# A tuned gated-convolution and two-MLP kernel on one core: other PSUM banks for transposes, later places for splits, sums and one block's convolution

## The chip, the cores and the metric

The kernel runs on one core of one Trainium2 chip. The metric is the time of one execution on the device in microseconds, smaller being better. Times are medians over several runs. The engines are PE (TensorE, matrix products and transposes), ACT (ScalarE), DVE (VectorE), POOL (GpSimd) and SP (SyncE, which issues the transfers).

## The reference

There are 8192 tokens (2 sequences of 4096) of 192 channels. Three steps follow one another, all in float32:

```python
# 1. dynamic convolution: 8 heads of 24 channels, 7 taps, weights by softmax over the taps
w = exp(weight_gen - max); w = w / (sum(w) + 1e-9)
x = einsum('bshk,bskhg->bshg', w, x_unfolded)       # this token and the 6 before it
# 2. layer 1: RMS norm, gated MLP, d_ff 1536
xn = x / sqrt(mean(x * x) + 1e-6) * rms_g
g = xn @ w_gate
y = (g * sigmoid(g) * (xn @ w_val)) @ w_out
# 3. layer 2: MLP, d_ff 2048
h = y @ w_in
z = (h * sigmoid(1.702 * h)) @ w_out
```

## The kernel before

The tokens are worked in 16 blocks of 512. For each block the program does the convolution with tokens on the partitions (on DVE, 13 operations over 128x768 elements, prepared by the softmax, whose exponential runs on ACT), the norm, and a transpose to channels on the partitions (TensorE, against an identity). Both MLPs then run with channels on the partitions.

Each float32 factor is split into a high and a low part of the shorter type fp32r (`h` and `l`; for x and y `xh`, `xl`, and for channels 128 to 191 `xsh`, `xsl`), and products are sums of several matmuls. Each matmul covers 64 rows of the array, and matmuls of the upper and of the lower rows go in pairs, side by side. The weights are split on the chip in the early part ("decode", lines 82 to 121).

The work is cut into **units**. Unit (1,b,m) makes 128 hidden columns of layer 1 for block b: it fills the PSUM banks `pg` and `pv`, ACT computes silu of `pg` into `p` (L401), DVE multiplies it with `pv` (L405), ACT casts the product to `h` (L406), DVE subtracts to get `l` (L409). Layer 1 has 12 such units per block. Unit (2,b,i) makes 256 hidden columns of layer 2: banks `ph` twice, ACT computes gelu of each to `h` (L422) and again to `p` (L423), DVE subtracts to `l` (L429). There are 8 per block. A unit's products with the second weights (D1 in layer 1, D2 in layer 2, each five matmul pairs) are added to the block's two sums `a` and `b` one or two units later, inside the matmul list of that later unit. A layer 1 unit so has nine pairs of its own and five for D1, 14; a layer 2 unit nine and ten, 19.

PSUM has 8 banks. Four form the pool `pu`, tag "u", for units and for the x transposes, so that a bank comes round after two units. The other four form `pacc`, for the sums: tags "a" and "b", two buffers each. When a bank passes from one row half to the other, an empty instruction on POOL relays the word (L331).

**Y(b)** takes layer 1's finished sums out of PSUM and splits them into `yh`, `yl`, `ysh`, `ysl`, the input of layer 2: four operations on ACT (L455 to L460) and three on DVE (L458, L459, L461). **Z(b)** takes out layer 2's sums and sends them to memory.

From block 2 on the order of units is: (1,b,4) to (1,b,11), then (1,b+1,0) to (1,b+1,3), then (2,b,0) to (2,b,7). At unit (1,b,10) the transposes of x(b+1) are issued, Y(b) falls to unit (1,b+1,1) and Z(b) to (1,b+1,5). Blocks 0 and 1 are interleaved. Block 14's layer 1 sums end, and all of block 15's layer 1 runs, ahead of block 14's layer 2.

Each engine works through its instructions in the order of the program. The first 24 units (AUTO) are ordered by the framework's scheduler, the rest stand as they are written. Convolution and weight decode are cut into small steps with costs and due times, and `some` deals them out between the parts of a unit:

```python
            for f in after:
                f()
            todo = [share(k, i) / 2 for k in (0, 1)]
            some(todo)
            second()
            some(todo)
            third()
```

`after` holds Y or Z. `second` is, in layer 1, product and cast, and `third` the subtraction; in layer 2 they are the two subtractions.

## Time and profile before

| | |
|---|---|
| median of 3 runs | 1325.36 us (1324.98 to 1326.92) |
| profiled execution | 1325.58 us, of which the span of instructions 1323.8 us |
| busy share of the span | PE 94%, DVE 60%, ACT 52%, POOL 2% |
| mean granted clock of TensorE | 0.988 |
| chain that ended last | PE 78%, DVE 12%, ACT 6% |

The busy share counts the time in which an engine has an instruction at work. The chain follows the work back from the last instruction, each step to what released it. The granted clock is a share of 2.4 GHz; 0.5 is the lower level, 1.2 GHz. In timeline rows a bracket gives how long the engine stood idle ahead of the instruction and what it waited for.

### The profile page before, as it was taken

What the parts mean: (1) busy time and instruction counts of PE and PEld (TensorE: products, weight loads), DVE (VectorE), ACT (ScalarE), POOL (GpSimd) and SP (SyncE); (2) the same over time, 40 slices, a digit from 0 to 9 for tenths busy, and PEclk for the clock granted to TensorE, in tenths of its full rate; (3) what the DMA queues carried; (4) which work ended last, traced back from release to release, by engine and by line L of the source; (5) the groups of instructions that cost most, each with busy time, mean ns of one, the idle gap of its engine ahead of it and who ended that gap; (6) DMA issues with size and microseconds to landing.
All of it is one profiled execution on the core that took longest, in us unless ns stands there. A gap on an engine that the chain in (4) does not pass through costs nothing.

```text
span 1323.8 us, 26554 instructions
## 1 busy us (share of the span) xinstructions
PE 1243.9 (94%) x10472; PEld 1131.5 (85%) x10472; DVE 788.7 (60%) x1286; ACT 691.8 (52%) x1350; POOL 31.5 (2%) x52
## 2 busy tenths in 40 slices
PE   1778899999999999999999999999999999999998
PEld 0567798889899898989989898998989899898897
DVE  8996575766655656565565656555466655645332
ACT  3564565465554555555555555545554555554453
POOL 3000000000000000000000000000000000000000
PEclk9989899999999999999999999999999999999999
DMA  6672121001001010100101000010100001000000
GB/s 232 218 241 86 54 67 65 32 1 43 2 1 53 1 43 1 43 2 1 53 2 43 1 26 18 1 54 1 43 1 12 32 1 44 1 13 2 1 14 12
DMA packets 16812, 51.70 MB, mean 39 GB/s; under 512 B 2096, under 2 KB 2480, under 8 KB 16560
## 3 DMA queue, kind: packets, MB, share of 16 engines
q1 hardware_dynamic: 16688, 50.01, 11.6%
q8 instruction: 82, 1.34, 0.4%
q14 instruction: 42, 0.34, 0.1%
HBM read 43.71 MB, written 6.29 MB: 38 GB/s over the span
## 4 chain that ended last, share of the span: by engine, by line
PE 78%; DVE 12%; ACT 6%; issue 2%; DMA 1%; POOL 0%; DVEq 0%; SPq 0%; POOLq 0%
PE a L316 21%; PE ph L316 18%; PE b L316 14%; PE pv L316 14%; PE pg L316 12%; DVE p L405 3%; DVE xr L229 2%; DVE acc L237 2%; ACT h L406 1%; ACT L422 1%; ACT h L422 1%; DVE dec_a L105 1%; DVE yt L458 1%; DVE ysl L461 1%; ACT ysh L460 1%
## 5 line engine op out<-in xcount | busy, mean ns | idle before, releaser
L316 PE MATMUL a<-h,o 64*128 64x512 f32 x1792 | 526.4, 395 | 4.2 <-POOLq L331 3.9
L316 PEld LDWEIGHTS a<-h,o 64*128 64x128 f32 x1792 | 330.2, 186 | 18.7 <-ACT p L401 4.2
L316 PE MATMUL b<-h,o 64*128 64x512 f32 x896 | 316.5, 397 | 9.3 <-ACT h L422 9.3
L316 PE MATMUL a<-l,o 64*128 64x512 f32 x896 | 318.1, 397 | 7.3 <-DVE l L429 7.2
L316 PE MATMUL b<-l,o 64*128 64x512 f32 x896 | 313.6, 395 | 2.8 <-DVE l L409 2.8
L429 DVE TENSOR_TENSOR l<-p,h 128x512 fp32r<-128x512 f32 x256 | 176.5, 690 | 221.7 <-ACT p L423 221.3
L422 ACT ACTIVATE h<-ph 128x512 fp32r<-128x512 f32 x256 | 153.5, 600 | 239.0 <-PE ph L316 237.0
L316 PE MATMUL pv<-xh,w 64*128 64x512 f32 x768 | 246.6, 401 | 17.1 <-DVE p L405 15.7
L316 PE MATMUL pg<-xh,w 64*128 64x512 f32 x768 | 254.2, 403 | 6.4 <-ACT xh L298 3.9
L316 PE MATMUL ph<-yh,w 64*128 64x512 f32 x1024 | 251.5, 395 | 0.0
L406 ACT CAST h<-p 128x512 fp32r<-128x512 f32 x192 | 119.0, 620 | 178.8 <-DVE p L405 178.8
L405 DVE TENSOR_TENSOR p<-p,pv 128x512 f32<-128x512 f32 x192 | 131.4, 684 | 111.0 <-PE a L316 77.9
L409 DVE TENSOR_TENSOR l<-p,h 128x512 fp32r<-128x512 f32 x192 | 132.8, 692 | 102.4 <-ACT h L406 102.4
L401 ACT ACTIVATE p<-pg 128x512 f32<-128x512 f32 x192 | 114.5, 597 | 149.0 <-PE pg L316 87.1
L316 PEld LDWEIGHTS b<-h,o 64*128 64x128 f32 x896 | 166.2, 186 | 20.1 <-ACT h L422 14.6
L316 PEld LDWEIGHTS a<-l,o 64*128 64x128 f32 x896 | 166.9, 186 | 17.1 <-DVE l L429 12.9
L316 PEld LDWEIGHTS b<-l,o 64*128 64x128 f32 x896 | 166.6, 186 | 10.5 <-DVE l L409 4.3
L316 PEld LDWEIGHTS pv<-xh,w 64*128 64x128 f32 x768 | 139.1, 187 | 36.7 <-DVE p L405 30.5
L316 PE MATMUL ph<-yl,w 64*128 64x512 f32 x512 | 163.7, 394 | 0.0
L316 PEld LDWEIGHTS ph<-yh,w 64*128 64x128 f32 x1024 | 152.6, 186 | 12.6 <-issue 0.2
L316 PEld LDWEIGHTS pg<-xh,w 64*128 64x128 f32 x768 | 142.0, 187 | 16.9 <-ACT xh L298 4.7
L423 ACT ACTIVATE p<-ph 128x512 f32<-128x512 f32 x256 | 152.4, 595 | 0.0
(81 smaller groups left out, 2211.8 us busy)
## 6 DMA issues: line engine op xcount, KB each, us to landing
x<-in_xp SPq DMA_DIRECT2D x14, 960.0 KB, 4.9
st<-in_w SPq DMA_DIRECT2D x20, 384.0 KB, 3.9
zt<-in_w SPq DMA_DIRECT2D x20, 384.0 KB, 3.8
st<-in_wo SPq DMA_DIRECT2D x14, 384.0 KB, 3.5
zt<-in_wo SPq DMA_DIRECT2D x14, 384.0 KB, 3.8
out_z<-za SPq DMA_DIRECT2D x16, 256.0 KB, 2.0
out_z<-zb SPq DMA_DIRECT2D x16, 128.0 KB, 2.3
x<-in_xp SPq DMA_DIRECT2D x1, 1344.0 KB, 5.9
```

The lines of the kernel that those rows point to most:

```text
L105: nc.vector.scalar_tensor_tensor(out=ai, in0=ai, scalar=3, in1=t["s"], op0=ALU.logical_shift_left, op1=ALU.bitwise_or)
L229: eng.tensor_tensor(out=dst.rearrange("p (q g) -> p q g", g=GRP), in0=x[:, k * D + a * GRP:k * D + e * GRP].rearrange("p (q g) -> p q g", ...
L237: eng.tensor_tensor(out=total[:, r], in0=total[:, r], in1=prod[:, r], op=ALU.add)
L316: ins = nc.tensor.matmul(ps[:, :N], w[rows], x[rows, :N], start=start, stop=stop)
L401: nc.scalar.activation(out=p[:, :N], in_=pg[:, :N], func=AF.Silu)
L405: nc.vector.tensor_tensor(out=p[:, :N], in0=p[:, :N], in1=pv[:, :N], op=ALU.mult)
L406: nc.scalar.copy(h[:, :N], p[:, :N])
L409: nc.vector.tensor_tensor(out=l[:, :N], in0=p[:, :N], in1=h[:, :N].bitcast(F32), op=ALU.subtract)
L422: nc.scalar.activation(out=h[:, :N], in_=ps[j][:, :N], func=AF.Gelu_apprx_sigmoid)
L423: nc.scalar.activation(out=p[:, :N], in_=ps[j][:, :N], func=AF.Gelu_apprx_sigmoid)
L429: nc.vector.tensor_tensor(out=l[:, :N], in0=p[:, :N], in1=h[:, :N].bitcast(F32), op=ALU.subtract)
L458: nc.vector.tensor_tensor(out=t[:, :N], in0=t[:, :N], in1=pb[:, :N], op=ALU.add)
```

## The change

- The four banks of the sums get fixed tags `a0`, `b0`, `a1`, `b1` by the parity of the block (`sums`), and the x transposes write there (`ax_`, `bx_`) instead of into unit banks.
- `transpose_x` issues the transposes at once and returns the split (4 ACT and 4 DVE operations, 2 and 2 for the first blocks), which comes behind the unit's product, cast and subtraction. So do Y and Z. Block 1's split stays where it was.
- From block 2 on, D2(b,0), layer 2's first sums, come one unit later: unit (2,b,1) has 14 pairs, (2,b,2) has 24. In the last unit of all, D2(13) is taken in rather than done alone after it.
- Block 2's x load, softmax and convolution start at unit (1,1,6) instead of (1,1,0).
- Block 0's convolution is no longer shared with POOL (SHARED): DVE does 768 elements instead of 624.
- Z's copy of `a` goes from DVE to ACT.

```diff
 
 BLOCKS = [4] * 16
 GROUPS = [(0, 1), (1, 2), (2, 4), (4, 7), (7, 10), (10, 13), (13, 16)]
-SHARED = {0: 6}
+SHARED = {}
 AHEAD = 4
 LAG = 6
 LAG2 = 3
...
     stg = early.enter_context(tc.tile_pool(name="stg", bufs=NST))
     dec = early.enter_context(tc.tile_pool(name="dec", bufs=3))
     pu = ctx.enter_context(tc.tile_pool(name="pu", bufs=4, space=PSUM))
-    pacc = ctx.enter_context(tc.tile_pool(name="pacc", bufs=2, space=PSUM))
+    pacc = ctx.enter_context(tc.tile_pool(name="pacc", bufs=1, space=PSUM))
 
     ident = const.tile([P, P], F32, name="ident")
     half = const.tile([P, TM], F32, name="half")
...
         xrow[b] = xr
         return ops
 
+    def sums(b, nm):
+
+        return [pacc.tile([P, NM], F32, tag=f"{n}{b % 2}", name=f"{n}{nm}{b}") for n in "ab"]
+
     def transpose_x(b, halves=False):
 
 
...
         l = xtp.tile([P, NM], F32R, tag="xl", name=f"xl{b}")
         sh = xtp.tile([P, NM], F32R, tag="xsh", name=f"xsh{b}")
         sl = xtp.tile([P, NM], F32R, tag="xsl", name=f"xsl{b}")
-        pa = pu.tile([P, NM], F32, tag="u", name=f"pa{b}")
-        pb = pu.tile([P, NM], F32, tag="u", name=f"pb{b}")
+        pa, pb = sums(b, "x_")
+        xT[b] = (h, l, sh, sl)
         if halves:
 
             for c in range(2):
...
                 for j in range(T):
                     nc.tensor.transpose(ps[:, j * P:(j + 1) * P], xr[:, j, c * P:(c + 1) * P], ident)
             parts = [(c, ps[:, :N], None) for c, ps in enumerate((pa, pb))]
-        for c, ps, i in parts:
-            h_, l_ = ((h, l), (sh, sl))[c]
-            h_, l_ = h_[:, :N], l_[:, :N]
-            if i is not None:
-                h_, l_ = (v.rearrange("p (j i t) -> p j i t", i=2, t=DR)[:, :, i] for v in (h_, l_))
-            nc.scalar.activation(out=h_, in_=ps, func=AF.Identity, scale=gt[:, c:c + 1])
-            nc.vector.scalar_tensor_tensor(out=l_, in0=ps, scalar=gt[:, c:c + 1],
-                                           in1=h_.bitcast(F32), op0=ALU.mult, op1=ALU.subtract)
-        xT[b] = (h, l, sh, sl)
+
+        def split():
+            for c, ps, i in parts:
+                h_, l_ = ((h, l), (sh, sl))[c]
+                h_, l_ = h_[:, :N], l_[:, :N]
+                if i is not None:
+                    h_, l_ = (v.rearrange("p (j i t) -> p j i t", i=2, t=DR)[:, :, i] for v in (h_, l_))
+                nc.scalar.activation(out=h_, in_=ps, func=AF.Identity, scale=gt[:, c:c + 1])
+                nc.vector.scalar_tensor_tensor(out=l_, in0=ps, scalar=gt[:, c:c + 1],
+                                               in1=h_.bitcast(F32), op0=ALU.mult, op1=ALU.subtract)
+        return split
 
 
     parts = [(sph, spl)]
...
 
     def D1(b, m):
         if m == 0:
-            acc1[b] = (pacc.tile([P, NM], F32, tag="a", name=f"a1_{b}"),
-                       pacc.tile([P, NM], F32, tag="b", name=f"b1_{b}"))
+            acc1[b] = sums(b, "1_")
         return (acc1[b], O1[m], m, M1, BLOCKS[b] * P, hl1.pop((b, m))), (lambda: Y(b)) if m == M1 - 1 else None
 
     def D2(b, m):
         if m == 0:
-            acc2[b] = (pacc.tile([P, NM], F32, tag="a", name=f"a2_{b}"),
-                       pacc.tile([P, NM], F32, tag="b", name=f"b2_{b}"))
+            acc2[b] = sums(b, "2_")
         return (acc2[b], O2[m], m, M2, BLOCKS[b] * P, hl2.pop((b, m))), (lambda: Z(b)) if m == M2 - 1 else None
 
     def Y(b):
...
         za = zp.tile([P, NM], F32, tag="za", name=f"za{b}")
         zb = zp.tile([P, NM], F32, tag="zb", name=f"zb{b}")[0:DR]
         nc.scalar.copy(zb[:, :N], pb[DR:P, :N])
-        nc.vector.tensor_copy(za[:, :N], pa[:, :N])
+        nc.scalar.copy(za[:, :N], pa[:, :N])
         nc.vector.tensor_tensor(out=zb[:, :N], in0=zb[:, :N], in1=pb[0:DR, :N], op=ALU.add)
         c = T0[b] * P
         nc.sync.dma_start(out=out[0:P, c:c + N], in_=za[:, :N])
...
         conv[14][1]()
         first[-1]()
         run(conv[15:])
-        transpose_x(0)
+        transpose_x(0)()
         for f in line.popleft()[0]:
             f()
         sm[2] = softmax_load(2)
...
             add_work(0, max(0, p - LOOK), [(2150, piece_steps)])
         nxt = 1
         ex_hook = None
+        start_at = None
         for i, u in enumerate(units):
             kind, b, m = u
             if (kind, b, m) == (1, 2, 0):
...
             if i == AUTO:
                 order.enter_context(tc.manual_schedule())
             run_work(i)
+            late = []
             if i in xt_by_pos:
-                transpose_x(nxt, nxt > 2)
+                split = transpose_x(nxt, nxt > 2)
+                if nxt == 1:
+                    split()
+                else:
+                    late.append(split)
                 nxt += 1
-                if nxt < NB:
-                    load_x(nxt)
-                    end = xt_at[nxt]
-                    gi = group_of.get(nxt)
-                    if gi is not None and gi >= 2:
-                        pr, ex_hook, post_ops = softmax_ops(gi, sm[gi])
-                        ex_at = next(j for j in range(i, len(units)) if units[j][0] == 2 and units[j][2] == 0)
-                        ex_at = i + 4 if gi == 2 else ex_at
-                        add_work(1, ex_at, pr)
-                    else:
-                        add_work(1, end - 2, conv_ops(nxt))
-                    gi = group_of.get(nxt + 1)
-                    if gi is not None and gi >= 2:
-                        sm[gi] = softmax_load(gi)
+                if nxt == 2:
+                    start_at = pos[1, 1, LAG]
+                elif nxt < NB:
+                    start_at = i
+            if i == start_at:
+                load_x(nxt)
+                end = xt_at[nxt]
+                gi = group_of.get(nxt)
+                if gi is not None and gi >= 2:
+                    pr, ex_hook, post_ops = softmax_ops(gi, sm[gi])
+                    ex_at = next(j for j in range(i, len(units)) if units[j][0] == 2 and units[j][2] == 0)
+                    ex_at = i + 4 if gi == 2 else ex_at
+                    add_work(1, ex_at, pr)
+                else:
+                    add_work(1, end - 2, conv_ops(nxt))
+                gi = group_of.get(nxt + 1)
+                if gi is not None and gi >= 2:
+                    sm[gi] = softmax_load(gi)
             if ex_hook and i == ex_at:
                 ex_hook()
                 ex_hook = None
...
                 downs.append(d)
                 after += [f] if f else []
             second, third = (U1 if kind == 1 else U2)(b, m, lambda *ups: matmuls(ups, downs, kind == 2 and b < 2))
-            for f in after:
-                f()
             todo = [share(k, i) / 2 for k in (0, 1)]
             some(todo)
             second()
             some(todo)
             third()
+            for f in late + after:
+                f()
             if kind == 1:
                 pend.append((i + 2, D1, (b, m)))
             else:
 
-                pend.append((i + 1, D2, (b, 2 * m)))
-                pend.append((i + 2 if b > 1 else i + 1, D2, (b, 2 * m + 1)))
+                last = len(units) - 1
+                pend.append((i + 2 if b > 1 and m == 0 else i + 1, D2, (b, 2 * m)))
+                pend.append((i + 1 if b < 2 or i + 1 == last else i + 2, D2, (b, 2 * m + 1)))
         while pend:
             _, D_, key = pend.popleft()
             d, f = D_(*key)
```

Three places show how instructions move. The line numbers after are those of the changed file: L405 becomes L411, L409 L415, L298 L304, L299 L305, L455 to L461 L459 to L465, L429 L435.

First, DVE around Y(7), the place of unit (1,8,1). Before:

```order
L237 TENSOR_TENSOR acc9_8598<-acc9_8598,xr9_8599 128x768
L409 TENSOR_TENSOR l1_8_0_8730<-p1_8_0_8728,h1_8_0_8729 128x512
L458 TENSOR_TENSOR yt7_8780<-yt7_8780,b1_7_7730 128x512
L459 TENSOR_TENSOR yl7_8777<-a1_7_7729,yh7_8776 128x512
L461 TENSOR_TENSOR ysl7_8779<-yt7_8780,ysh7_8778 128x512
L405 TENSOR_TENSOR p1_8_1_8772<-p1_8_1_8772,pv8_1_8737 128x512
L409 TENSOR_TENSOR l1_8_1_8774<-p1_8_1_8772,h1_8_1_8773 128x512
L229 TENSOR_TENSOR xr9_8599<-x9_8596,wraw4_5406 128x768
L405 TENSOR_TENSOR p1_8_2_8827<-p1_8_2_8827,pv8_2_8794 128x512
```

and now:

```order
L237 TENSOR_TENSOR acc9_8577<-acc9_8577,xr9_8578 128x768
L415 TENSOR_TENSOR l1_8_0_8717<-p1_8_0_8715,h1_8_0_8716 128x512
L411 TENSOR_TENSOR p1_8_1_8759<-p1_8_1_8759,pv8_1_8724 128x512
L415 TENSOR_TENSOR l1_8_1_8761<-p1_8_1_8759,h1_8_1_8760 128x512
L462 TENSOR_TENSOR yt7_8770<-yt7_8770,b1_7_7717 128x512
L463 TENSOR_TENSOR yl7_8767<-a1_7_7716,yh7_8766 128x512
L465 TENSOR_TENSOR ysl7_8769<-yt7_8770,ysh7_8768 128x512
L229 TENSOR_TENSOR xr9_8578<-x9_8575,wraw4_5385 128x768
L411 TENSOR_TENSOR p1_8_2_8814<-p1_8_2_8814,pv8_2_8781 128x512
```

Y's three additions (`yt7`, `yl7`, `ysl7`) stood ahead of the product `p1_8_1` and now stand behind its subtraction, with an operation of block 9's convolution (L229) between them and the next product. On ACT Y's four operations move likewise from ahead of the cast `h1_8_1` to behind it, and so stand ahead of the silu `p1_8_2`.

Second, ACT around the split of x(8), the place of unit (1,7,10). Before:

```order
L406 CAST h1_7_9_8560<-p1_7_9_8559 128x512
L298 ACTIVATE xh8_8566<-pa8_8570,gt_105 128x4x64
L298 ACTIVATE xh8_8566<-pb8_8571,gt_105 128x4x64
L298 ACTIVATE xsh8_8568<-pa8_8570,gt_105 128x4x64
L298 ACTIVATE xsh8_8568<-pb8_8571,gt_105 128x4x64
L401 ACTIVATE p1_7_10_8640<-pg7_10_8604 128x512
L406 CAST h1_7_10_8641<-p1_7_10_8640 128x512
```

and now:

```order
L412 CAST h1_7_9_8547<-p1_7_9_8546 128x512
L407 ACTIVATE p1_7_10_8619<-pg7_10_8583 128x512
L412 CAST h1_7_10_8620<-p1_7_10_8619 128x512
L304 ACTIVATE xh8_8553<-ax_8_8557,gt_105 128x4x64
L304 ACTIVATE xh8_8553<-bx_8_8558,gt_105 128x4x64
L304 ACTIVATE xsh8_8555<-ax_8_8557,gt_105 128x4x64
L304 ACTIVATE xsh8_8555<-bx_8_8558,gt_105 128x4x64
L407 ACTIVATE p1_7_11_8671<-pg7_11_8635 128x512
```

The four `xh8` and `xsh8` stood ahead of the silu `p1_7_10`, now they stand behind its cast and ahead of the silu `p1_7_11`; they read sums' banks. On DVE the four `xl8` and `xsl8` move from behind `l1_7_9` to behind `l1_7_10`.

Third, DVE at the start of layer 2, where Y(1) and the decode of a weight (`dec_a`, `dec_s`, `w2_4`) meet the subtractions of units (2,0,1) and (2,0,2). Before:

```order
L429 TENSOR_TENSOR l2_0_0_1701<-p2_0_0_1699,h2_0_0_1700 128x512
L429 TENSOR_TENSOR l2_0_1_1706<-p2_0_1_1704,h2_0_1_1705 128x512
L458 TENSOR_TENSOR yt1_1800<-yt1_1800,b1_1_830 128x512
L459 TENSOR_TENSOR yl1_1797<-a1_1_829,yh1_1796 128x512
L461 TENSOR_TENSOR ysl1_1799<-yt1_1800,ysh1_1798 128x512
L105 SCALAR_TENSOR_TENSOR dec_a_1718<-dec_a_1718,dec_s_1720 128x384
L109 TENSOR_SCALAR dec_s_1720<-dec_a_1718 128x384
L115 SCALAR_TENSOR_TENSOR w2_4_1545<-zt_1547,dec_s_1720 128x384
L99 TENSOR_SCALAR dec_s_1820<-st_1607 128x384
L101 TENSOR_SCALAR zt_1608<-zt_1608 128x384
L429 TENSOR_TENSOR l2_0_2_1788<-p2_0_2_1786,h2_0_2_1787 128x512
L229 TENSOR_TENSOR xr2_947<-x2_725,wraw2_225 128x768
L429 TENSOR_TENSOR l2_0_3_1793<-p2_0_3_1791,h2_0_3_1792 128x512
L429 TENSOR_TENSOR l2_0_4_1874<-p2_0_4_1872,h2_0_4_1873 128x512
```

and now:

```order
L435 TENSOR_TENSOR l2_0_0_1682<-p2_0_0_1680,h2_0_0_1681 128x512
L229 TENSOR_TENSOR xr2_1534<-x2_1300,wraw2_212 128x768
L435 TENSOR_TENSOR l2_0_1_1687<-p2_0_1_1685,h2_0_1_1686 128x512
L105 SCALAR_TENSOR_TENSOR dec_a_1699<-dec_a_1699,dec_s_1701 128x384
L109 TENSOR_SCALAR dec_s_1701<-dec_a_1699 128x384
L115 SCALAR_TENSOR_TENSOR w2_4_1519<-zt_1521,dec_s_1701 128x384
L99 TENSOR_SCALAR dec_s_1790<-st_1585 128x384
L101 TENSOR_SCALAR zt_1586<-zt_1586 128x384
L435 TENSOR_TENSOR l2_0_2_1770<-p2_0_2_1768,h2_0_2_1769 128x512
L237 TENSOR_TENSOR acc2_1533<-acc2_1533,xr2_1534 128x768
L435 TENSOR_TENSOR l2_0_3_1775<-p2_0_3_1773,h2_0_3_1774 128x512
L462 TENSOR_TENSOR yt1_1800<-yt1_1800,b1_1_813 128x512
L463 TENSOR_TENSOR yl1_1797<-a1_1_812,yh1_1796 128x512
L465 TENSOR_TENSOR ysl1_1799<-yt1_1800,ysh1_1798 128x512
L435 TENSOR_TENSOR l2_0_4_1856<-p2_0_4_1854,h2_0_4_1855 128x512
```

Y(1) (`yt1`, `yl1`, `ysl1`) moves from ahead of `l2_0_2` to behind `l2_0_3`. The decode stays ahead of `l2_0_2`, and two operations of block 2's convolution (`xr2`, `acc2`) now stand here. Further ahead, before the product `p1_0_9`, one operation of that convolution is left on DVE of the seven before.

## Rows read from the trace of the kernel before

**Rows 1.** Windows: length, busy us (instructions) of each engine, clock, DMA share, GB/s.
```profile
110.00:151.60 41.60, 41.25 (x355) 35.31 (x357) 19.18 (x29) 22.25 (x38) 0.00 (x0) 1.00 0.05 17
151.60:162.70 11.10, 7.04 (x41) 5.43 (x39) 8.98 (x18) 5.98 (x14) 0.00 (x0) 0.71 0.23 71
208.53:214.82 6.29, 6.19 (x51) 4.91 (x47) 3.96 (x6) 3.58 (x8) 0.00 (x0) 1.00 0.60 191
1247.00:1257.00 10.00, 7.87 (x54) 6.26 (x52) 4.58 (x7) 4.12 (x8) 0.00 (x0) 0.83 0.00 0
```

**Rows 2.** Waits of all engines by releaser: us in total, times, longest us.
```profile
DVE yt L458 <- ACT yt L456: 31.6, 13, 4.3
...
PE b L316 <- ACT h L422: 9.3, 12, 1.2
```

**Rows 3.** Timeline at Y(7), unit (1,8,1): start us, us, engine, line, [idle before].
```profile
660.38 0.60 ACT L401 ACTIVATE p<-pg 128x512 f32<-128x512 f32 x1 [1.28 <-PE pg L316]
...
662.21 0.69 DVE L458 TENSOR_TENSOR yt<-yt,b 128x512 f32<-128x512 f32 x1 [2.29 <-ACT yt L456]
...
663.92 0.39 PE L316 MATMUL pg<-xh,w 64*128 64x512 f32 x1
664.20 0.68 DVE L405 TENSOR_TENSOR p<-p,pv 128x512 f32<-128x512 f32 x1
...
664.93 0.50 PE L316 MATMUL pv<-xh,w 64*128 64x512 f32 x1 [0.62 <-DVE p L405]
```

**Rows 4.** Timeline behind the transposes of x(8), ahead of unit (1,7,10).
```profile
647.08 0.47 PE L316 MATMUL pg<-xh,w 64*128 64x512 f32 x1
...
647.69 0.50 PE L316 MATMUL pv<-xh,w 64*128 64x512 f32 x1
...
649.96 0.49 DVE L299 SCALAR_TENSOR_TENSOR xsl<-pa,gt,xsh 128x256 fp32r<-128x256 f32 x1
```

**Rows 5.** Timeline from unit (2,7,1) to (2,7,2).
```profile
671.33 0.83 PE L316 MATMUL ph<-yh,w 64*128 64x512 f32 x4
...
673.99 0.62 ACT L423 ACTIVATE p<-ph 128x512 f32<-128x512 f32 x1
...
676.84 0.63 PE L316 MATMUL ph<-yh,w 64*128 64x512 f32 x3
```

**Rows 6.** Timeline from unit (2,8,1) to (2,8,2), an Exp ahead of it.
```profile
748.84 0.84 PE L316 MATMUL ph<-yh,w 64*128 64x512 f32 x4
...
752.18 0.62 ACT L423 ACTIVATE p<-ph 128x512 f32<-128x512 f32 x1
...
755.03 0.84 PE L316 MATMUL ph<-yh,w 64*128 64x512 f32 x4
```

**Rows 7.** Timeline of block 0's convolution, DVE and POOL.
```profile
15.13 0.88 POOL L229 TENSOR_TENSOR xr<-x,wraw 128x144 f32<-128x144 f32 x1
...
16.36 1.08 DVE L237 TENSOR_TENSOR acc<-acc,xr 128x624 f32<-128x624 f32 x1
...
17.36 0.59 DVE L99 TENSOR_SCALAR dec_s<-st 128x384 int32<-128x384 int32 x1
...
20.35 0.80 DVE L229 TENSOR_TENSOR xr<-x,wraw 128x624 f32<-128x624 f32 x1
...
23.24 0.35 DVE L99 TENSOR_SCALAR dec_s<-st 128x384 int32<-128x384 int32 x1
```

**Rows 8.** Timeline around an operation of block 2's convolution.
```profile
104.81 0.95 DVE L229 TENSOR_TENSOR xr<-x,wraw 128x768 f32<-128x768 f32 x1
...
106.42 0.50 PE L316 MATMUL pv<-xh,w 64*128 64x512 f32 x1 [2.90 <-DVE p L405]
...
106.75 0.39 PE L316 MATMUL pv<-xh,w 64*128 64x512 f32 x1
```

**Rows 9.** Timeline of the last groups of sums, each alone.
```profile
1314.87 0.47 PE L316 MATMUL a<-h,o 64*128 64x512 f32 x1 [0.20 <-POOLq L331]
...
1317.07 0.47 PE L316 MATMUL a<-h,o 64*128 64x512 f32 x1 [0.20 <-POOLq L331]
```

## The prediction

> **What bounds the kernel now.** I read the page's busy shares and windows first: in an undisturbed stretch, 110.00 to 151.60 us, TensorE is busy 41.25 of 41.60 us, DVE and ACT about half [rows 1]. So the time is TensorE's work plus its gaps, and the change is worth the gaps that it closes. Nothing in it alters the number of matmuls. Next come the waits, grouped by who waits for whom: the reader is to see two that recur once a block, Y's first addition behind ACT's copies (13 times) and a matmul on sum `b` behind a gelu (12 times) [rows 2]. The timelines of one such place each then show what a gap costs, and windows do so for the irregular beginning and end.
>
> For the windows I need a pace. In that stretch 355 matmuls fill 41.60 us, 0.1172 us each [rows 1]. A unit of layer 1 (14 pairs, 28 matmuls) is then 3.28 us, one of layer 2 (19 pairs) 4.45 us. What a stretch takes beyond that is lost.
>
> **Y after the unit's activations.** Before, Y stands ahead of the product of unit (1,b+1,1). ACT starts that unit's silu at 660.38, DVE waits with `yt` until 662.21, and the product L405 comes at 664.20, although silu was over at 660.98. TensorE wants its `pv` bank for the next unit but one: `pg` goes at 663.92 and `pv` only at 664.93 [rows 3]. That is 1.01 us where 0.12 is due: 0.89 lost, 13 times, 11.6 us.
>
> After, the product goes at once (661.0 to 661.7), cast and subtraction follow, then Y. What is late next is the silu of unit (1,8,2), queued behind Y's four copies on ACT. I take every ACT step at the silu's 0.60 and each DVE step at `yt`'s 0.69, issued about 0.6 apart [rows 3]: cast to 662.3, two copies to 663.5, `yh` to 664.1, `yt` on DVE 663.5 to 664.2, `ysh` to 664.9, silu to 665.5. DVE ends `ysl` at 665.6, does one convolution operation of 0.95 [rows 8], and the product that frees the bank ends near 667.15. Unit (2,7,0) wants it one unit after 663.92, at 667.2 to 667.3. It fits by about 0.1. I count the 0.89 as gained whole; if the fit fails by some tenths, as much returns in each of the 13 blocks.
>
> **x: other banks, split later.** Before, the transposes take two banks of the units. The first `pg` is at 647.08, the first `pv` at 647.69 because its bank waits for a product [rows 4]: 0.61 for 0.12, of which I count 0.43, since that `pg` had started while transposes still ran. With the sums' banks this wait has no cause. Blocks 3 to 15: 13 x 0.43 = 5.6 us. The transposes themselves remain.
>
> The split now follows the subtraction of unit (1,7,10). With U its start, silu is at U+3.0 (660.38 is 3.54 ahead of 663.92 [rows 3], which lies two units, 6.55, after that unit's start), product, cast and subtraction end near U+5.7, four DVE operations of at most 0.49 [rows 4] end at U+7.6. Unit (1,8,0), two units later, reads `xsl` in its sixth pair: U + 6.55 + 5 x 0.23 = U+7.7. Again it fits by 0.1 to 0.2, so nothing is counted.
>
> **Layer 2's first sums one unit later.** Before, unit (2,b,1) starts at 671.33 and the next at 676.84: 5.51 for 4.45, 1.06 lost to the first gelu [rows 5]. In the four blocks where an Exp goes before, 748.84 to 755.03 is 6.19, 1.74 lost [rows 6]. After, (2,b,1) has 14 pairs and no need of a gelu, (2,b,2) has 24. But (2,b,1) ends 1.17 us sooner, and (2,b,2) needs both banks of (2,b,0) from its first pair, while the last gelu leaves its bank at 673.99 + 0.62 = 674.61, in the Exp block at 752.18 + 0.62 = 752.80 [rows 5, 6]. TensorE arrives 3.28 after the start, at 674.61 and 752.12. What stays is next to nothing, which I set at 0.2 for the restart, and 0.7 in the Exp blocks. Sum: 8 x (1.06 - 0.2) + 4 x (1.74 - 0.7) = 11.0 us.
>
> **Block 0's convolution on DVE alone.** While POOL works, 624 elements take DVE 1.08 us, later 0.80; a decode step 0.59, later 0.35 [rows 7]. Without POOL the same operation has 768 elements and takes 0.95 [rows 8]. Eight operations ran slowed: 8 x 0.28 = 2.2 gained; 13 x 0.15 = 2.0 lost; some seven decode steps between them gain 0.24 each, 1.7. That makes 1.9 at best and, if the decode is hidden, 0.2; I take 1.0.
>
> The page "SBUF — State Buffer" of the Trainium skill (section "SBUF: two separate sides") has GpSimd and a DVE operation with two SBUF inputs take an exclusive lock for a whole instruction, so that the loser fully blocks. By it eight DVE operations would have stood up to 0.88 each, the POOL operation's length [rows 7], and the start would give 7.0 instead of 2.2 for them, the forecast 1277. The rows show 0.28 per operation and DVE and POOL at work side by side, so they set the price; the case is in rival 3.
>
> **Block 2's convolution later.** Its load and six of seven early operations leave the stretch ahead of unit (1,0,9). There TensorE waits 2.90 us for a product that stands behind one such operation of 0.95 [rows 8]. Six at about 0.87 are 5.2 us of DVE work. The softmax stays early, and weights are still decoded there, so less than all is gained: I take 3.1 (2.9 and the restart), between 0 and 5.2. The work goes into layer 2's units.
>
> **Start of layer 2.** The window from 151.60 to 162.70 holds 41 matmuls, 4.8 us of work in 11.1, at a mean granted clock of 0.71, partly on the 1.2 GHz level [rows 1]. DVE does Y(1) and a weight's decode ahead of `l2_0_2`. After, `l2_0_2` and `l2_0_3` come ahead of Y(1), and Y(1) ahead of `l2_0_4`. 6.3 is the most to gain; I leave 1.2 for the new wait behind Y(1) and take 5.1 (3 to 6.3). A new wait of some 2 us could bring a lower clock again. The page "TensorE: Matmul & The Clock Gate" (section "What's actually happening") of the Trainium skill says that the throttled state is the default and activity releases it. The rows agree in part: this wait came with 0.71, while the one of 2.90 at 106.42 was followed by matmuls as fast as before [rows 1, 8].
>
> **Z and x(2), early.** The window at 208.53, a 19-pair unit and block 2's transposes, takes 6.29 where the unit alone is 4.45 [rows 1]: up to 1.8 lost. `za` moves from DVE to ACT, Z and the split behind the activations: I take 1.5.
>
> **The end.** From 1247 to 1257, 54 matmuls take 10.0 us instead of 6.3, clock 0.83: Y(15) ahead of unit (2,14,2)'s subtraction [rows 1]. After, Y(15) comes behind it: 3.7. D2(13) moves from a group alone (1314.87 to 1317.07, 2.20 us) [rows 9] into the last unit, where its five pairs cost 1.17: 1.0. Together 4.7. The last `za` copy now stands behind `zb` on ACT, under 0.1.
>
> **Sum.** 11.6 + 5.6 + 11.0 + 1.0 + 3.1 + 5.1 + 1.5 + 4.7 = 43.6. The profiled execution took 1325.58 us, 0.2 above the median shown, so the sum holds for both: **1282 us**. 0.2% (2.7 us) is about what a measurement of this kernel tells from no change.
>
> **Rivals.**
> 1. *The first sums' gap only moves.* (2,b,2) is the heaviest unit, 24 pairs, and needs the banks in its first pair. For: the fit is exact in [rows 5], and any delay of the gelus by the cast of (1,b+1,3) shows at once. Against: that cast no longer stands behind a delayed product. At 0.9 per block all 12 gains vanish: 1293. Chance 0.12.
> 2. *A split or Y that comes just too late.* Both margins are 0.1 to 0.2 from rounded steps. If `xsl` or `pv` misses by 0.5 in 13 blocks, 6.5 returns, by both 13: 1288 to 1295. Chance 0.15.
> 3. *The early part gives little.* DVE's decode and softmax may remain the limit, and convolution 2 is only moved into layer 2, where DVE then delays subtractions. Of 10.7 perhaps 2 is kept: 1291. Chance 0.10. Its mirror image, where the whole early gain comes (1.9, 5.2, 6.3, 1.8), gives 1277.5, chance 0.08.
> 4. *Slower.* ACT is held by Y and by the split for 2.4 and 1.9 us in a unit of 3.28, in which it also has silu and cast (1.2): it is over its unit by 0.3 at Y. If the lateness didn't decay but passed through product, subtraction and D1 into the next units, each block would lose what the next silus are late. It decides against the change from 43.6 / 13 = 3.4 us per block on; 3.7 gives 1330. Against: ACT's next unit has only 1.2 us of work in 3.28, which takes up 2 us of lateness per unit. Chance 0.03.
> 5. *The change doesn't do what it says at block 2*: the first 24 units are ordered by the scheduler, which may pull the convolution forward. The order shows one operation there and not seven, so this is counted inside 3.
>
> The forecast has 0.52. The range reaches from the full early gain, less another 7 for terms sized too small (1270), to rivals 1 and 2 (1295); it leaves out under 0.2. The cases below no change make 0.96, within 0.2% 0.01, above 0.03.
>
> **What would show it.** Right: no `pv` waiting for a product at Y and none after the transposes; Y(7)'s additions on DVE behind the subtraction of (1,8,1); the time from one (2,b,1) to the next, 671.33 to 748.84 [rows 5, 6], down from 77.5 by 0.89 + 0.43 + 0.86 to 75.3; units (2,b,1) at 3.3 and (2,b,2) at 5.6 to 6.3 us; no clock under 1.00 near 1250. Wrong: a new wait of TensorE for `p` or `xsl` in every block; a gap at the first pair of (2,b,2) over 0.9; a later first matmul; or a longer stretch ahead of unit (2,0,2).

## The result and the profile after

| | before | changed |
|---|---|---|
| median | 1325.21 us (4 runs, 1324.98 to 1326.92) | 1285.46 us (4 runs, 1284.05 to 1287.72) |
| profiled execution | 1325.58 us, span 1323.8 us | 1284.05 us, span 1282.0 us |

The ratio is 0.9699, 95% interval 0.9682 to 0.9716: 39.8 us faster. The forecast was 1282 us, 43.6 us less, in a range from 1270 to 1295. The profiled executions lie 41.5 us apart, mostly since the changed kernel's is the fastest of its four.

The page's line of busy times after the change:

```profile
PE 1227.0 (96%) x10472; PEld 1163.0 (91%) x10472; DVE 777.8 (61%) x1270; ACT 696.7 (54%) x1366; POOL 21.4 (2%) x39
```

The same 10472 matmuls are busy 16.9 us less, although none was taken out. In part this is the lower clock, at which a matmul takes longer: 0.79 us behind a wait in the run e1, 0.50 at the same place here. The rest of the 41.8 us of span were gaps.

The waits of all engines after (us in total, times, longest us), which answer to [rows 2]:

```profile
DVE yt L462 <- ACT yt L460: 5.7, 12, 0.5
PE pv L322 <- DVE p L411: 5.6, 6, 2.4
...
PE ph L322 <- ACT p L429: 1.0, 4, 0.3
```

`yt` waits 5.7 us in 12 places where it was 31.6 in 13. The six waits of `pv` all lie ahead of 101 us, so no `pv` waits at a Y or behind the transposes of a later block. TensorE's wait for the gelu `h` ahead of sum `b` (9.3 us in 12 places) has no row any more. What took its place is the third row: the first matmul of unit (2,b,2) on a bank that a gelu still reads, in the four blocks with an Exp, 1.0 us of idle time in all.

Y(7) after, timeline from the silu of unit (1,8,1) on (start, length, engine, line, in brackets the idle time before). It answers to [rows 3]:

```profile
640.12 0.60 ACT L407 ACTIVATE p<-pg 128x512 f32<-128x512 f32 x1 [1.15 <-PE pg L322]
...
640.75 0.69 DVE L411 TENSOR_TENSOR p<-p,pv 128x512 f32<-128x512 f32 x1 [0.97 <-PE a L322]
...
643.32 0.69 DVE L462 TENSOR_TENSOR yt<-yt,b 128x512 f32<-128x512 f32 x1 [0.51 <-ACT yt L460]
...
644.57 0.59 ACT L407 ACTIVATE p<-pg 128x512 f32<-128x512 f32 x1
...
645.30 0.95 DVE L229 TENSOR_TENSOR xr<-x,wraw 128x768 f32<-128x768 f32 x1
...
646.17 0.68 DVE L411 TENSOR_TENSOR p<-p,pv 128x512 f32<-128x512 f32 x1
...
646.99 0.47 PE L322 MATMUL ph<-yh,w 64*128 64x512 f32 x2
```

The product L411 goes 0.63 us after its silu began, where L405 came 3.82 after. Y stands behind it, the next silu is late (644.57, 4.45 behind the one before, in a unit of 3.25), and the next product, behind a convolution operation, ends at 646.85. The bank is wanted by unit (2,7,0), which starts on time at 646.99. That is the fit "by about 0.1" of the prediction: 0.14.

x(8), answering to [rows 4]:

```profile
627.39 0.48 PE L322 MATMUL pg<-xh,w 64*128 64x512 f32 x1
...
627.46 0.48 PE L322 MATMUL pv<-xh,w 64*128 64x512 f32 x1
```

0.07 us lie between the first `pg` and the first `pv`, 0.61 before. Layer 2's first units, answering to [rows 5] and [rows 6]:

```profile
650.25 0.70 PE L322 MATMUL ph<-yh,w 64*128 64x512 f32 x4
...
653.11 0.62 ACT L429 ACTIVATE p<-ph 128x512 f32<-128x512 f32 x1
...
653.50 0.78 PE L322 MATMUL ph<-yh,w 64*128 64x512 f32 x3
...
653.78 0.30 PEld L322 LDWEIGHTS ph<-yh,w 64*128 64x128 f32 x3 [0.32 <-ACT p L429]
```
```profile
725.61 0.73 PE L322 MATMUL ph<-yh,w 64*128 64x512 f32 x4
...
728.80 0.62 ACT L429 ACTIVATE p<-ph 128x512 f32<-128x512 f32 x1
728.87 0.40 PE L322 MATMUL ph<-yh,w 64*128 64x512 f32 x1
...
729.47 0.30 PEld L322 LDWEIGHTS ph<-yh,w 64*128 64x128 f32 x3 [0.65 <-ACT p L429]
```

Unit (2,b,1) takes 3.25 us. The second bank of (2,b,2) comes free when the last gelu ends, at 653.73, and its weight load starts at 653.78; with an Exp ahead at 729.42 and 729.47, 0.65 late. From one (2,b,1) to the next it is now 75.36 us, 77.51 before; 75.3 was forecast.

To see where the time came from, I read in both traces when a unit's first matmul starts.

| up to the start of | before | changed | gained in the stretch | forecast |
|---|---|---|---|---|
| (1,1,4): POOL's share, convolution 2 | 113.49 | 110.62 | 2.9 | 4.1 |
| (2,1,1): start of layer 2 | 177.43 | 169.82 | 4.7 | 5.1 |
| (1,2,9): Z and x(2) | 254.02 | 245.40 | 1.0 | 1.5 |
| (2,14,0): 12 to 13 blocks of x, Y and first sums | 1238.34 | 1202.14 | 27.6 | 28.2 |
| the end of the span | 1323.8 | 1282.0 | 5.6 | 4.7 |

The first row is one execution's, and a good one. Five runs below (e1, e2, e3, e4, e8) have the same instructions in the same order on ACT and DVE up to (1,1,4), and reach it at 113.34, 114.69, 111.33, 111.19 and 110.82 us: between 1.2 later and 2.7 earlier than the kernel before.

Windows of the changed kernel (length, then busy time and instructions of PE, PEld, DVE, ACT, POOL, then clock, DMA share, GB/s): from unit (1,0,7) up to (1,1,4), then up to (2,0,1), up to (2,1,1), and units (2,14,1) to (2,14,3). The last two answer to the second and fourth of [rows 1].

```profile
78.22:110.62 32.40, 26.22 (x200) 20.01 (x197) 26.67 (x62) 17.37 (x33) 0.00 (x0) 1.00 0.68 225
110.62:143.22 32.60, 32.60 (x283) 29.24 (x281) 15.62 (x23) 15.77 (x26) 0.00 (x0) 1.00 0.01 1
143.22:169.82 26.60, 24.48 (x203) 22.66 (x201) 22.55 (x41) 18.92 (x40) 0.00 (x0) 1.00 0.44 134
1205.39:1218.65 13.26, 13.26 (x117) 13.19 (x115) 6.70 (x10) 9.81 (x20) 0.00 (x0) 1.00 0.01 1
```

By the pace of 0.1172 us a matmul the first holds 23.4 us of work in 32.40, so 9.0 are still lost there; the second loses nothing; the third 2.8 of 26.60; the fourth, 3.7 before, nothing. (A window counts matmuls that only overlap its edges; by whole units the losses are up to 0.5 larger, 9.4 and 3.2 here.) The clock is 1.00 in all four.

### The profile page after: what moved, and what is told of

Same layout as the page of the kernel before. It is cut to its first block, busy times and chain, and to the rows that moved or that the text cites. A ratio compares the mean times of both kernels' runs of the same rounds, so it can differ in the third digit from the quotient of the medians.

```text
span 1282.0 us, 26559 instructions
## 1 busy us (share of the span) xinstructions
PE 1227.0 (96%) x10472; PEld 1163.0 (91%) x10472; DVE 777.8 (61%) x1270; ACT 696.7 (54%) x1366; POOL 21.4 (2%) x39
## 3 DMA queue, kind: packets, MB, share of 16 engines
HBM read 43.71 MB, written 6.29 MB: 39 GB/s over the span
## 4 chain that ended last, share of the span: by engine, by line
PE 88%; DVE 7%; ACT 2%; DMA 1%; issue 1%; POOL 0%; SPq 0%; POOLq 0%; DVEq 0%
PE a L322 23%; PE ph L322 19%; PE pg L322 16%; PE b L322 15%; PE pv L322 14%; DVE acc L237 1%; DVE xr L229 1%; DVE dec_a L105 1%; DVE p L411 1%; DMA zt<-in_wo 1%; DVE l L435 0%; DVE dec_s L99 0%; DVE dec_s L109 0%; DMA x<-in_xp 0%; DVE l L415 0%
## 5 line engine op out<-in xcount | busy, mean ns | idle before, releaser
L322 PE MATMUL a<-l,o 64*128 64x512 f32 x896 | 314.2, 395 | 2.7 <-DVE l L435 2.6
L322 PE MATMUL b<-h,o 64*128 64x512 f32 x896 | 312.6, 395 | 0.0
L435 DVE TENSOR_TENSOR l<-p,h 128x512 fp32r<-128x512 f32 x256 | 175.9, 690 | 212.4 <-ACT p L429 210.7
L322 PE MATMUL pg<-xh,w 64*128 64x512 f32 x768 | 246.2, 399 | 6.7 <-ACT xh L304 3.4
L322 PE MATMUL ph<-yh,w 64*128 64x512 f32 x1024 | 245.1, 395 | 1.0 <-ACT p L429 1.0
L411 DVE TENSOR_TENSOR p<-p,pv 128x512 f32<-128x512 f32 x192 | 131.7, 686 | 148.8 <-PE a L322 116.7
L415 DVE TENSOR_TENSOR l<-p,h 128x512 fp32r<-128x512 f32 x192 | 132.8, 692 | 103.3 <-ACT h L412 103.3
L322 PEld LDWEIGHTS ph<-yh,w 64*128 64x128 f32 x1024 | 150.0, 185 | 13.2 <-ACT p L429 5.2
L322 PE MATMUL ph<-yl,w 64*128 64x512 f32 x512 | 158.7, 392 | 0.0
L429 ACT ACTIVATE p<-ph 128x512 f32<-128x512 f32 x256 | 153.9, 601 | 0.5 <-DVE l L435 0.5
L322 PE MATMUL pg<-xl,w 64*128 64x512 f32 x384 | 151.6, 395 | 0.0
```

The costliest lines, as they stand in the source:

```text
L322: ins = nc.tensor.matmul(ps[:, :N], w[rows], x[rows, :N], start=start, stop=stop)
L411: nc.vector.tensor_tensor(out=p[:, :N], in0=p[:, :N], in1=pv[:, :N], op=ALU.mult)
L415: nc.vector.tensor_tensor(out=l[:, :N], in0=p[:, :N], in1=h[:, :N].bitcast(F32), op=ALU.subtract)
L429: nc.scalar.activation(out=p[:, :N], in_=ps[j][:, :N], func=AF.Gelu_apprx_sigmoid)
L435: nc.vector.tensor_tensor(out=l[:, :N], in0=p[:, :N], in1=h[:, :N].bitcast(F32), op=ALU.subtract)
```

## The experiments

Ratios are to the kernel before, run beside each on the same chip, with medians of 1325.08 to 1325.95 us. Differences are those of the medians to the changed kernel's 1285.46, which was not run beside them; by the ratios they come out up to 0.9 us otherwise (e5 -0.1, e6 -1.7, e8 -3.3). An interval is some 2 us to either side, so a difference under 2 decides nothing by itself; then the trace does.

| run | median, us | ratio, interval | to the changed kernel |
|---|---|---|---|
| e1_d2_back | 1296.23 | 0.9777, 0.9763 to 0.9792 | +10.8 |
| e2_y_back | 1295.04 | 0.9769, 0.9754 to 0.9784 | +9.6 |
| e3_split_early | 1284.26 | 0.9686, 0.9672 to 0.9701 | -1.2 |
| e4_x_back | 1290.76 | 0.9734, 0.9718 to 0.9751 | +5.3 |
| e5_conv2_back | 1284.48 | 0.9698, 0.9683 to 0.9712 | -1.0 |
| e6_auto18 | 1282.90 | 0.9686, 0.9672 to 0.9701 | -2.6 |
| e7_auto12 | 1280.57 | 0.9668, 0.9652 to 0.9684 | -4.9 |
| e8_exp_early | 1281.49 | 0.9674, 0.9660 to 0.9688 | -4.0 |
| e9_pool_shared | 1286.05 | 0.9708, 0.9691 to 0.9724 | +0.6 |
| e10_early_all | 1278.88 | 0.9654, 0.9639 to 0.9668 | -6.6 |
| e11_exp2_at_gelu | 1276.87 | 0.9640, 0.9625 to 0.9654 | -8.6 |
| e12_conv2_spread | 1275.91 | 0.9633, 0.9616 to 0.9649 | -9.6 |

My theory was the prediction's: each gap has one cause of its own (a bank, an order, a gelu), and undoing that part brings that gap back. The rivals: the gaps had moved, or another part had closed them.

### e1_d2_back: first sums in unit (2,b,1) again

```diff
-                pend.append((i + 2 if b > 1 and m == 0 else i + 1, D2, (b, 2 * m)))
+                pend.append((i + 1, D2, (b, 2 * m)))
```

> The changed kernel with layer 2's first sums D2(b,0) back in unit (2,b,1). My account: unit (2,b,1) takes 19 pairs again and waits for the first gelu, 1.1 us in eight blocks and 1.7 to 1.8 in the four with an Exp, and the 0.2 and 0.9 that unit (2,b,2) shows after the change goes away. Per block 0.9, so 10 to 11.5 us slower than the changed kernel. Rival (the gap had only moved): within 2 us of the changed kernel.

10.8 us slower, and the row is back, with more than the 9.3 of before:

```profile
PE b L322 <- ACT h L428: 12.3, 12, 1.3
```

The gap had not only moved.

### e2_y_back: Y ahead of the product again

```diff
+            if kind == 1 and b > 2 and m == 1:
+                while after:
+                    after.pop(0)()
             todo = [share(k, i) / 2 for k in (0, 1)]
```

> The changed kernel with Y(2) to Y(14) issued again ahead of the product of unit (1,b+1,1); Y(0), Y(1), Y(15), Z and the split stay late. My account: pv of unit (1,b+1,3) waits again 0.86 to 0.95 us in 13 blocks: 11.6 us slower. Rival (the sums' banks or the Z order had removed it): within 2 us.

9.6 us slower. The wait is there as in [rows 3], `pv` of unit (1,8,3) behind the product:

```profile
651.22 0.39 PE L322 MATMUL pg<-xh,w 64*128 64x512 f32 x1
651.72 0.68 DVE L411 TENSOR_TENSOR p<-p,pv 128x512 f32<-128x512 f32 x1
...
652.45 0.49 PE L322 MATMUL pv<-xh,w 64*128 64x512 f32 x1 [0.84 <-DVE p L411]
```

1.23 us lie between `pg` and `pv`, the most of the 13. In the trace these units lose 0.7 to 1.1, together 10.9. Less than that came back because what TensorE loses there ACT gains: unit (2,7,2), 5.74 us long in the changed kernel, takes 5.60 here, and the eight units (2,b,2) without an Exp are 1.3 us shorter together.

### e3_split_early and e4_x_back: the bank or the place of the split

```diff
-                if nxt == 1:
+                if nxt == 1 or nxt > 2:
                     split()
```

> The changed kernel with the split of x(3) to x(15) issued right behind the transposes, ahead of the unit's silu, while the transposes stay in the sums' banks. My account: the 0.4 us behind the transposes came from the units' banks alone, so this changes nothing: within 1 us of the changed kernel. Rival (the later place of the split is what gains): 5 to 6 us slower.

e4 has the same line, and the transposes in unit banks:

```diff
-        pa, pb = sums(b, "x_")
+        if halves:
+            pa, pb = [pu.tile([P, NM], F32, tag="u", name=f"p{n}{b}") for n in "ab"]
+        else:
+            pa, pb = sums(b, "x_")
```

> The changed kernel with the transposes of x(3) to x(15) in two unit banks again and the split right behind them, so the whole part on x undone for these blocks. My account: pv behind the transposes waits again, 13 times 0.4 us: 5 to 6 us slower. Rival (the place of the split, not the banks): the same here, so this run counts only beside the one with the early split.

1.2 us faster and 5.3 slower. In e3 the first `pg` and `pv` start 0.11 us apart:

```profile
627.72 0.47 PE L322 MATMUL pg<-xh,w 64*128 64x512 f32 x1
...
627.83 0.47 PE L322 MATMUL pv<-xh,w 64*128 64x512 f32 x1
```

In e4:

```profile
629.93 0.48 PE L325 MATMUL pg<-xh,w 64*128 64x512 f32 x1
...
630.50 0.49 PE L325 MATMUL pv<-xh,w 64*128 64x512 f32 x1
```

It is 0.57 us, and e4 is 6.5 us slower than e3, from which only the banks differ. So the whole gain on x comes from the banks. The later split gains nothing with these banks, and costs nothing that the runs can tell.

### e5_conv2_back and e9_pool_shared: the two early edits

```diff
-                    start_at = pos[1, 1, LAG]
+                    start_at = i
```

> The changed kernel with block 2's load, softmax and convolution started at unit (1,1,0) again. The step of the prediction: the convolution's six operations stand ahead of unit (1,0,9) again, 3.1 us slower. Account from the trace of the changed kernel: there units (1,1,2) and (1,0,9) still lose 2.7 and 3.2 us, to softmax and weight decode that moved up into the room, so the later start gained little there, about 1.4 us; and layer 2's first units lose 0.5 to 1 us less without the convolution. Within 1.5 us of the changed kernel.

```diff
-SHARED = {}
+SHARED = {0: 6}
```

> The changed kernel with block 0's convolution shared with POOL again (624 elements on DVE, 144 on POOL). The prediction's step: 1.0 us slower, 0.2 to 1.9; the traces of the kernels without POOL show the first transposes 1.0 to 1.5 us earlier than before. By the exclusive-lock account, in which DVE stands for whole POOL operations, some 6 us slower.

1.0 us faster and 0.6 slower: neither edit by itself can be told from nothing. The windows from unit (1,0,7) up to (1,1,4) of e5, of e9, and of e1, whose instructions stand here in the same order as the changed kernel's:

```profile
77.36:113.33 35.97, 28.40 (x200) 22.31 (x198) 32.75 (x72) 16.77 (x34) 0.00 (x0) 0.91 0.71 226
```
```profile
79.47:113.46 33.99, 29.12 (x199) 22.46 (x197) 27.20 (x64) 17.71 (x34) 0.00 (x0) 0.85 0.67 221
```
```profile
79.05:113.34 34.29, 29.24 (x200) 23.08 (x197) 26.48 (x61) 17.33 (x33) 0.00 (x0) 0.84 0.63 210
```

In e5 DVE has 32.75 us of work where it was 26.67, and the stretch is 3.6 us longer than the changed kernel's 32.40, but e1 is 1.9 longer there too with no other order, at a clock of 0.84. The changed kernel's profiled execution happens to have no lower clock here. Its four runs point the same way: 1284.05 us at a mean clock of 0.993, 1285.23 at 0.991, 1285.69 at 0.990, 1287.72 at 0.989. Single traces of this stretch therefore differ by more than these edits are worth, and the medians decide: about nothing for convolution 2, and for POOL's share 0.6, which is within the interval.

### e6_auto18 and e7_auto12: what fills DVE early

```diff
-AUTO = 24
+AUTO = 18
```

(12 in e7.)

> The changed kernel with the scheduler's part ending at unit 18 instead of 24, so that from unit (1,1,6) on everything stands as written. The decode of four weights (w2_2, o2_2, w2_3, o2_3), block 2's softmax and its first convolution operation, about 12 us of DVE work, then come in or behind units (1,1,6) to (2,0,0), where TensorE never waits, and not ahead of unit (1,0,9). Account (work pulled forward fills DVE while TensorE waits for products): 5 to 9 us faster than the changed kernel. Rival (the early waits come from transfers, POOL and block 1's convolution): within 1 us.

> As the run before, with the scheduler's part ending at unit 12: the decode of w1_11, w2_0, o2_0, w2_1 and o2_1 too then stands in units (1,0,9) to (1,1,5), one piece of 2.1 us in a unit of 3.26. Account: another 3 to 6 us faster than with 18, unless a weight comes later than its unit. Rival: no faster than with 18, since block 1's convolution and its transposes are the limit ahead of unit (1,1,0).

2.6 and 4.9 us faster, both less than stated. The two windows of e7: from unit (1,0,7) up to (1,1,5), and from (1,1,9) up to (2,0,2).

```profile
78.07:107.35 29.28, 29.28 (x255) 28.45 (x253) 17.26 (x33) 13.43 (x26) 0.00 (x0) 1.00 0.28 86
120.36:145.81 25.45, 21.07 (x163) 15.40 (x161) 20.64 (x44) 17.37 (x31) 0.00 (x0) 1.00 0.43 126
```

The first shows 255 matmuls in 29.28 us: TensorE is never short, where the changed kernel lost 9.0. So the work that was pulled forward is the cause, as the account had it; which part of it is not told, since the edit moves decode, softmax and the Exp of twelve units at once. In the second 163 matmuls take 25.45 instead of 19.1: 6.3 us are lost again. A silu there waits for block 2's Exp and two table loads, and layer 2's first subtractions stand behind decode and convolution. The two rivals, which expected nothing, fall by the trace: e6 starts unit (1,1,4) at 103.90 and e7 at 100.84, where the changed kernel does at 110.62. My sum had left out what the moved work does where it goes.

### e8_exp_early: the Exp away from the gelus

```diff
...
+            if i in soon:
+                gi = soon[i]
+                pr, soon_hook, soon_post = softmax_ops(gi, sm[gi])
+                add_work(0, i + 3, pr)
+            if soon_hook and i - 3 in soon:
+                run_work(i)
+                soon_hook()
+                soon_hook = None
...
```

> The changed kernel with the first softmax steps and the Exp of blocks 4, 7, 10 and 13 moved from ahead of layer 2's first gelu to unit (1,b,7) of the same block, between a cast and a silu. Account (the 0.8 to 1.1 us that unit (2,b,2) loses in these four blocks is the Exp and its table load ahead of the gelus): these four lose 0.2 like the others, 2.5 to 3 us faster in all. Rival (the silu behind the Exp comes 2 us late and pv waits there): no gain, or up to 2 us slower.

4.0 us faster. Unit (2,8,2) there:

```profile
726.98 0.62 ACT L429 ACTIVATE p<-ph 128x512 f32<-128x512 f32 x1
...
727.17 1.21 PE L322 MATMUL ph<-yh,w 64*128 64x512 f32 x4
...
727.65 0.29 PEld L322 LDWEIGHTS ph<-yh,w 64*128 64x128 f32 x3 [0.53 <-ACT p L429]
```

The last gelu ends at 727.60, 0.43 after the unit's first matmul, and the unit is 5.93 us long instead of 6.67. The four such units are 2.4 us shorter together, near the 2.5 to 3 that was stated, though they still lose 0.3 each and not 0.2; the rest of the 4.0 is within the interval. The silu behind the Exp was late, and no `pv` waited for it in any of the four blocks. The rival falls.

### e10, e11, e12: the early part put together

e10 is AUTO = 12, the Exps as in e8, and block 2 started at (1,1,3); e11 is the same with block 2 at (1,1,6) and without the line `ex_at = i + 4 if gi == 2 else ex_at`; e12 starts block 2 at (1,1,0).

> The run with the scheduler's part ending at unit 12 and the four Exps in unit (1,b,7), put together, and block 2's load, softmax and convolution started at unit (1,1,3), its Exp four units later at (1,0,11). In the run with 12 the trace shows 9.8 us gained by unit (1,1,9) and 6.6 lost again up to unit (2,0,1), behind a silu that waits for block 2's Exp and two table loads. Account: the Exp now meets units with less decode around it, so part of the 6.6 stays: 1272 to 1277 us. Rival (the Exp costs as much wherever it stands between silus): 1278, which is the run with 12 less 2.7.

> As the run before, but block 2 starts at unit (1,1,6) as in the changed kernel, and its Exp stands directly ahead of layer 2's first gelu, which saves one of the two table loads (the silu one). Account: no silu is late, so the 3 us lost at units (1,1,11) and (2,0,0) go; units (2,0,1) and (2,0,3) still lose 2 to 3 us each to subtractions behind decode and convolution: 1273 to 1277 us. Rival: the first gelu, now late by the Exp, costs as much as the silu did: 1278.

> The run with the scheduler's part ending at unit 12 and the four Exps in unit (1,b,7), with block 2 started at unit (1,1,0) as in the kernel before: its Exp falls into the scheduled part, ahead of unit (1,0,9), and its convolution is dealt out over units (1,0,9) to (2,1,4), one operation in most units, rather than over layer 2's alone. Account (what is lost from (1,1,9) to (2,0,4), 6 to 10 us in the two runs before, is block 2's Exp between silus and convolution and softmax ahead of layer 2's first subtractions): 1272 to 1276 us. Rival (from (1,0,9) on DVE has 1.2 for a unit, 2.1 for a decode and 0.9 for the convolution, 4.2 in 3.26, and TensorE waits there again): 1277 to 1281.

1278.88, 1276.87 and 1275.91. The time of e10 is the rival's, but the Exp between two silus is not the whole of it: units (1,1,8) and (1,1,9) lose 4.4 us, and in e12, whose Exp stands 37 us earlier, the same two lose 2.9, behind Y(0), a decode and a convolution operation on DVE. In e11 the Exp costs no silu, but (2,0,1) and (2,0,3) lose 4.0 and 3.7. The first waits 1.4 and 0.5 us for gelus that the Exp and its loads made late, as that run's rival had it, the second 1.9 us for a subtraction. In e12:

```profile
78.27:107.58 29.31, 29.31 (x255) 28.80 (x252) 19.05 (x37) 12.38 (x24) 0.00 (x0) 1.00 0.28 91
117.79:145.07 27.28, 24.32 (x193) 17.91 (x190) 23.44 (x46) 17.52 (x34) 0.00 (x0) 1.00 0.47 144
```

Nothing is lost up to (1,1,5), and 193 matmuls, 22.6 us, take 27.28 from (1,1,8) to (2,0,1): 4.7 lost. From the start of unit (1,0,7) to that of (2,1,1) e12 takes 86.95 us, the shortest of the four (e11 88.52, e7 88.78, e10 89.64). e12 beats both kernels: 49.2 us faster than before, 9.6 faster than the change. It is within 1 us of e11, which the intervals do not tell apart. From (1,1,9) to (2,0,4) it still loses 7.2 us (e7 9.9, e10 8.8, e11 9.6), so the waits behind DVE of its rival are there too, and account and rival, 1 us apart in time, are not decided.

## Why the prediction was right, and where it was not

**Y, right in mechanism and size.** The timeline followed the hand-made one within 0.1 us, slack included. e2 gives 9.6 for 11.6: by its trace the units at Y lose 10.9, 0.84 each where 0.89 was counted, and 1.3 comes back in the units (2,b,2).

**x, right.** 5.3 for 5.6 (e4), and e3 shows the cause, the bank, alone. That the split also moved was rightly counted as nothing.

**First sums, right.** 10.8 for 11.0 (e1). What stays in (2,b,2) was set at 0.2 and 0.7; the units there are 5.67 to 5.88 us long, and with an Exp 6.42 to 6.67, for 24 pairs, 5.63 by the pace: up to 0.3, and 0.8 to 1.0. The last passes the forecast's 6.3 for these units. That it is mostly the Exp was argued there, and is shown by e8.

**Start of layer 2: 4.7 for 5.1, with some luck.** Unit (2,0,2) takes 4.5 us where it took 11.1. The later convolution did not do this, since e5 has it back and takes 4.5 too; that leaves Y(1) behind `l2_0_3`, though no run puts Y(1) alone back. The size came out because two numbers were both too small. Units (2,0,2), (2,0,3), (2,1,0) and (2,0,4) lost 6.7, 0.1, 1.2 and 0.0 us by the pace, 8.0 together where 6.3 was counted; they lose 0.0, 1.9, 0.5 and 0.8 now, 3.2 where 1.2 was left. The new wait is in (2,0,3):

```profile
156.06 0.95 DVE L229 TENSOR_TENSOR xr<-x,wraw 128x768 f32<-128x768 f32 x1
...
156.93 0.68 DVE L435 TENSOR_TENSOR l<-p,h 128x512 fp32r<-128x512 f32 x1
...
157.67 0.50 PE L322 MATMUL a<-l,o 64*128 64x512 f32 x1 [1.56 <-DVE l L435]
```

It ends with a subtraction that stands behind a decode and an operation of block 2's convolution, and only further back behind Y(1). No lower clock came with it (1.00 in the window).

**Block 2's convolution later, wrong.** This is the step that failed: "less than all is gained: I take 3.1 (2.9 and the restart), between 0 and 5.2". The run that undoes it, e5, is no slower. The prediction looked at one wait and the operation ahead of it and took the room that the six operations left for gained. That wait, which stood in unit (1,1,3), is gone: the unit takes 3.25 us where it took 6.42, and 7.98 in e5. But (1,1,1) takes 4.31 for 3.25 and (1,0,9) 6.43 for 4.83, and the work that went into layer 2 shows there: units (2,1,0) and (2,0,4) take 4.92 and 5.27 us, 4.44 and 4.85 in e5. DVE did not come free. In the changed kernel it works without a gap for 15 us here:

```profile
88.10:103.10 15.00, 9.74 (x64) 5.91 (x62) 15.00 (x37) 8.78 (x16) 0.00 (x0) 1.00 0.90 299
```

The changed kernel also shows what stands in the room: block 2's Exp with two table loads is now here, on ACT, ahead of a silu,

```profile
92.37 1.28 ACT L184 ACT_TABLE_LOAD   x1
...
95.73 1.28 ACT L407 ACT_TABLE_LOAD   x1
...
99.86 0.68 DVE L411 TENSOR_TENSOR p<-p,pv 128x512 f32<-128x512 f32 x1
...
100.60 0.50 PE L322 MATMUL pv<-xh,w 64*128 64x512 f32 x1 [2.43 <-DVE p L411]
```

and the product at 99.86, behind softmax and decode steps, is what unit (1,0,9) waits for, 2.4 us. With both, and decode, taken out of this stretch (e7) the loss goes. In e5 the Exp stands ahead of unit (1,0,7) and the stretch loses no less, so the Exp's place alone is not it. The 3.1 us would be most of the 3.8 between forecast and median. By the table the traces fall only 1.8 short, 1.2 of it up to (1,1,4); the other 2.0 lie between profiled executions and medians, and that they too were lost in the early part, where executions of one order differ by 4 us, is likely but not shown.

**POOL's share: 0.6 for 1.0, which the runs cannot tell from nothing.** In the changed kernel operations of 768 elements take 0.95 and decode steps 0.35 from the beginning, as reckoned. From the first convolution operation to the first transposes it is 18.73 us (to 26.40), where it was 20.24 (to 27.89) and in e9 is 20.23. How much of these 1.5 is left at unit (1,1,4) the traces do not tell.

What the prediction said of POOL was misread. It took "DVE and POOL at work side by side" as speaking against a lock. The kernel before shows them in turn:

```profile
14.63 1.09 DVE L229 TENSOR_TENSOR xr<-x,wraw 128x624 f32<-128x624 f32 x1
...
15.64 0.79 DVE L115 SCALAR_TENSOR_TENSOR w<-zt,dec_s 128x384 fp32r<-128x384 int32 x1
16.10 0.68 POOL L237 TENSOR_TENSOR acc<-acc,xr 128x144 f32<-128x144 f32 x1
```

With POOL's 15.13 and DVE's 16.36 of [rows 7], they end one after the other: DVE at 15.72, POOL at 16.01, DVE at 16.43, POOL at 16.78, DVE at 17.44. Each of POOL's 13 operations ends 0.29 to 0.35 us after the DVE operation beside which it began, be its recorded length 0.48 or 1.03, so most of that length is waiting. DVE pays 0.24 to 0.29 per operation, not the 0.88 that the prediction put to the lock. So e9 does not speak against the exclusive lock that the page "SBUF — State Buffer" of the Trainium skill describes (section "SBUF: two separate sides"), only against the some 6 us. The rows agree with that page in that the two engines take turns; that a lock is the reason is not shown by any run here.

**Z and x(2): 1.0 for 1.5.** Unit (2,1,5) with block 2's transposes takes 5.67 us where it took 6.29. The prediction had counted the transposes' own time, which stays, as lost; another 0.4 came in unit (1,2,2). **The end: 5.6 for 4.7.** Units (2,14,2) and (2,14,3) lose nothing now, and nothing either in e1, so this is not the later first sums. A smaller stall in (2,15,2), 0.4 us, which I had not counted, went too.

**Rivals.** The first-sums gap did not move, the margins held, lateness of ACT did not pass into later units (the silu is 1.2 late at Y, and no later unit of the block waits), so none of the three that would have given the gain back, or turned it, happened. Rival 3, little from the early part, held for one of its four terms.

## What to carry to other kernels

Where the same gap returns once a block, follow the one bank or buffer from its last reader to its next writer, and step each engine's queue by hand with durations from the trace: that forecast 28.2 us here and 27.6 came, though the margins were 0.1. Where a stretch is bound by a queue that a scheduler fills, removing work from it is no gain until you have seen what moves up into its place. A part that can sit on either of two resources (transposes in the banks of the units or of the sums) belongs on the one whose next user is far away.
